# Row maxima 20 instead of 22 steps ahead of the scores, in an attention kernel with a dense gate

## The chip, the cores and the metric

The kernel runs on one core of one Trainium2 chip. The metric is the device time of one execution in microseconds. TensorE (PE), VectorE (DVE), ScalarE (ACT), GpSimd (POOL) and SyncE (SP, which only starts transfers here) have one instruction queue each, in program order.

## The reference

Attention with 32 query heads of 16 dimensions that share one key and value head, over a sequence of 2048, and beside it a layer of dense products with the Mish function; the output is a sum of x and the attention, gated.

```python
q = (x @ wq).reshape(B, S, H, Dh).transpose(0, 2, 1, 3)     # 32 heads, S = 2048, Dh = 16
k = x @ wk; v = x @ wv                                      # one head
p = softmax(einsum("bhqd,bkd->bhqk", q, k) * Dh ** -0.5)
o = einsum("bhqk,bkd->bhqd", p, v)                          # -> (S, 512) @ wo
h = einsum("bsd,df->bsf", x, w1) + b1                       # 512 -> 1792
act = h * tanh(softplus(h))                                 # Mish
y = einsum("bsf,fd->bsd", act, w2)                          # 1792 -> 512
```

A layernorm of x stands ahead of both, and the dense result passes a silu before it multiplies the attention's. All is float32, made of products of rounded high and low parts.

## The kernel before, in words

**Groups and steps.** The attention is cut into 32 groups `v` (four heads by 512 queries) of 16 steps each, `NS` = 512 steps in all. A step has four score products `e` (`score`, L1090), each followed by one exponential on ScalarE (`pts`, L1095), and four value products `pv` on the exponentials of the step before last (L1176; the profile counts eight matmuls for them). The scores use half of the array's rows at a time, half a=1 in even steps and a=0 in odd ones.

**Maxima.** The softmax needs the maximum of each row of scores before its exponentials. So the same scores are computed once more with queries and keys exchanged (`m_one`, matmul L1118), and VectorE takes the maximum of each 512 (reduce, L1122, into `mb`). A group has 64 such maxima products, 32 for each half of the array; each step carries four of them, for a later group. `LEAD` (L34) says how many steps they run ahead: ahead of the first score there must be 2 x `LEAD` maxima products on each half (L1436, and the end of the lead, L1498). `TAIL` = `NS` - `LEAD` is the step from which there are no maxima left. The tail takes the steps in pairs (`tail_pair`, L1590), with two dense groups side by side.

**The rows.** When a group's maxima are complete (`m_need`, L67), `c_rows` (L1134 to 1163) makes two more rows of its q tile out of them. It has pieces: a reduce (L1141), two small ones (`parts`), and a piece that transposes on VectorE (`turn`, L1151: `cr` out of `mp`) and then issues eight transfers of 2 KB on SyncE's queue (`move`, L1161: `qt<-cr`), four for half a=1 and then four for a=0. A group's first score (half a=1) waits for the first four, its fifth (the next step, half a=0) for the other four. `top_rows(n)` (L1567) queues up to n of these pieces: one behind each step, none behind a step that ended a dense group whose bank VectorE emptied (`top_rows(0 if evacs[0] else 1)`, L1733), two behind each half of a unit (L1679), three behind a pair of the tail (L1715).

**Dense work.** Beside these run dense products (queries of later groups, w1, w2, wo; L118 and L122, written to banks `xps`). Each is split into two halves of the array's rows, for two successive steps (`waves`): mostly six halves in a step, in some four or eight. A `unit` (L684) is four steps as two halves with a dense group of up to 16 products, ordered by the list `UNIT`.

**The lead.** All ahead of the first score is ordered by a planner (the loop of L1360 to 1560): it takes the task that can start first by its own costs, on each engine. `fill(n)` issues n dense products there, `keep_warm` a product whose result is not used; a task marked `fill` is preceded by such a product where no dense group is open. `cdone` is the time when the first group's rows are taken to be there, and ends the lead.

Of the kernel before, what the change touches and what calls it, by code (L numbers as in the profile page):

```python
# [30 lines left out]
NFT = F // P  # L31
NKT = S // P
NU = 8 * NC
LEAD = 22  # L34
NWARM = 24
E0 = 76.0
X_US = 9.0
# [91 lines left out]
def block_kernel(ctx: ExitStack, tc: tile.TileContext, x, wq, wk, wv, wo, w1, b1, w2, out):  # L129
# [10 lines left out]
    pe, act, dve, pool, sp = nc.tensor, nc.scalar, nc.vector, nc.gpsimd, nc.sync  # L140
# [46 lines left out]
    def f(ap):  # L187
        return ap.bitcast(F32)
# [354 lines left out]
    def pump():  # L543
        for tag in items:
            while arrived(tag):
                split(tag)
            for _ in range(2 if tag == "wb" else 1):
                load(tag)
# [135 lines left out]
    def unit(s, h):  # L684


        g, t = cur["g"], s + 2 * h
        xs = deque(g.mms)
        v, r = divmod(s, 16)
        es = deque((1 - h, r + j // 2, j % 2) for j in range(8))  # L690
        late = []
        relay = None

        def x_one():
            i = xs.popleft().half(cur["ps"], h)
            if len(xs) == len(g.mms) - 1 and h:
                tc.add_manual_dep(i.ins, cur["relay"].ins.name, mybir.DependencyInfo(
                    mybir.DependencyClass.Sync, mybir.DependencyReason.DATA), reason="other half of the bank")
            if h and g.dve and len(xs) == HOLD:
                held[0] = []  # L700
            if not xs and h:
                cur["n"] = len(g.mms)
                finish()
                for top in held[0] or ():
                    top()
                held[0] = None

        due(t)
        for n, op in enumerate(UNIT):
            if n == 8:  # L710
                due(t + 0.5)
                pump()
                due(t + 1)
            if xs:
                x_one()
            if op == "E":
                e = es.popleft()
                if len(es) > 1:
                    score(v, *e)()
                else:  # L720
                    late.append(score(v, *e))
            else:
                relay = m_one(1 - h)
        assert not xs and not es
        cur["relay"] = relay
        act_jobs(2 + (len(jobs) > 2))
        due(t + 1.5)
        for n in range(2):
            pv(t + n - 2)
            if n == 0:  # L730
                for fn in late:
                    fn()
        if t % 16 == 0:
            o_out((t - 16) // 16)
# [399 lines left out]
    def c_rows(v):  # L1134

        mp = sb.tile([P, 2, 3, 8], F32R, tag="mp", name=f"mp{v}", bufs=2)
        mx = f(mp[:, :, 0])
        w = {}

        def reduce():  # L1140
            dve.reduce_max(out=mx, in_=mb_of[v].rearrange("p b (a z) -> p a z b", a=2), axis=AX.X)  # L1141

        def parts():
            dve.tensor_reduce(out=mp[:, :, 1], in_=mx.rearrange("p a (z o) -> p a z o", o=1), axis=AX.X,
                              op=ALU.max, negate=True)
            dve.tensor_reduce(out=f(mp[:, :, 2]), in_=f(mp[:, :, 0:2]).rearrange("p a s z -> p a z s"), axis=AX.X,
                              op=ALU.add, negate=True)

        def turn():
            cr = w["cr"] = sb.tile([P, 32], F32, tag="cr", name=f"cr{v}", bufs=2)  # L1150
            dve.transpose(cr, f(mp[:, :, 1:3]).rearrange("p a s z -> p a (s z)"))  # L1151

        def move():
            q, cr = qt_of[v], w["cr"]
            if not lead:
                sp_t[0] = max(sp_t[0], us_of(step[0]) + 4.0)
            for a in range(1, -1, -1):
                r = 64 * a + 48
                for b in range(4):
                    sp_at(0.68)  # L1160
                    sp.dma_start(f(q[r:r + 2]).rearrange("o p (t b n) -> b o (p t) n", b=4, n=32)[b],  # L1161
                                 cr[32 * b + 16 * a:32 * b + 16 * a + 16])
        return reduce, parts, turn, move

# [102 lines left out]
    def due(t):  # L1267
        step[0] = t
        for k in sorted(k for k in timed if k <= t):
            for fn in timed.pop(k):  # L1270
                fn()
# [198 lines left out]
                   for d in k.deps)  # L1470

    begun = [0]
    cdone = [None]
    kind = [None]
    while True:
        opts = []
        for e in ("ACT", "DVE", "POOL", "SP"):
            if e == "POOL":
                T[e] = max(T[e], busy[0] + E0)
            if b := best(e):  # L1480
                early = max(now[0], b[1].start(0))
                opts.append((early if e == "DVE" and b[1].prio < 2 and b[0] < early + 5.0 else b[0], e, b[1]))
        b = best("PE")
        m = m_ready(T["PE"])
        if m is not None and b and b[0] < T["PE"] + 0.2 and T["DVE"] > T["PE"] + 1.0:
            m = None
        if m is not None and (b is None or m <= b[0] + 0.05 or T["DVE"] < T["PE"] + 0.3 and m <= T["PE"] + 0.1):
            opts.append((m, "PE", "M"))
        elif b:
            opts.append((b[0], "PE", b[1]))  # L1490
        e0 = min((o for o in opts if o[1] == "PE"), default=None, key=lambda o: o[0])
        low = min((o[0] for o in opts), default=None)
        if e0 is None or e0[0] > T["PE"] + 0.35:
            opts.append((T["PE"], "PE", "X"))
        if not any(o[1] == "ACT" and o[0] < T["ACT"] + 0.1 for o in opts):
            opts.append((T["ACT"], "ACT", "J"))
        s, e, k = min(opts, key=lambda o: o[0])
        if cdone[0] is not None and s >= cdone[0] - 0.4 and min(m_next) >= 2 * LEAD:  # L1498
            break
        when(s)  # L1500
        for tag in items:
            load(tag)
        if k == "M":
            d = max(T["DVE"], s + 0.45)
            for a in pick[0]:
                if m_next[a] == len(mseq):
                    mseq.append(pick[1])
                    got[pick[1][0]] += 1
                m_one(a)
                d += 0.6  # L1510
                m_ends.append(d)
            T["DVE"] = d
            T["PE"] = s + (0.25 if kind[0] == "M" else 0.45)
            kind[0] = "M"
            if vdone[0] == 0 and got[0] == 32 and m_next[0] == m_next[1]:
                vdone[0] = 1
                r = c_rows(0)
                r1 = task("DVE", 0.9, lambda: (r[0](), r[1](), r[2]()))

                def move():  # L1520
                    r[3]()
                    cdone[0] = now[0] + 4 * 0.65 + 2.0
                task("SP", 5.2, move, [r1])
        elif k == "X":
            fresh = cur["g"] is None
            if cur["g"] is not None or not waiting and (vdone[0] or begun[0] < 1 + (s - 18) / X_US) and begin():
                begun[0] += fresh
                fill(3)
                T["PE"] = s + 0.23 * 3 + (0.2 if kind[0] == "M" else 0)
                kind[0] = "X"  # L1530
            else:
                keep_warm()
                T["PE"] = s + 0.25
                kind[0] = "X"
        elif k == "J":
            tag = next((g for g in ("wq", "ws", "wb") if not any(soon(k, s) for k in plan["POOL"]) and arrived(g) and busy[0] + E0 < s + (4.5 if g == "ws" else 0.5)), None)
            n = ran[0]
            if tag:
                split(tag)
                T["ACT"] = s + 0.6  # L1540
            else:
                gap[0] = 0
                if not plan["POOL"]:
                    act_jobs(1)
                T["ACT"] = s + (0.65 if ran[0] > n else 0.15)
        else:
            plan[e].remove(k)
            if k.fill and cur["g"] is None and not waiting:
                keep_warm()
            k.fn()  # L1550
            T[e] = max(s, T[e]) + k.us + (0.15 if e == "PE" and kind[0] == "M" else 0)
            k.end = T[e]
            if e == "PE":
                kind[0] = "T"
# [117 lines left out]
    for s in range(NS + 2000):  # L1672
# [3 lines left out]
        if s % 4 == 0 and s + 4 <= NS - LEAD and unit_ready(s):  # L1676
            for h in range(2):
                unit(s, h)
                top_rows(2)  # L1679
                evacs[0] = 0  # L1680
                pump()
            base[:] = s + 4, us_of(s) + UNIT_US
            skip[0] = s + 4
            continue
# [66 lines left out]
```

## Time and profile before

| | |
|---|---|
| runs | 1563.36, 1560.67, 1563.7 us (median 1563.36) |
| the profiled execution | 1561.58 us |
| its span | 1559.8 us |
| TensorE busy | 1548.8 us (99%), mean granted clock 0.998 |
| VectorE, ScalarE, GpSimd busy | 1348.1, 1292.6, 636.3 us |
| first score of the attention | 80.23 us after the span's start |

The span is what the profile covers; 1.8 us of the execution lie around it. In a row of the profile stand the time or number, the engine, the kernel's line, the operation, and the tiles, output first (`e<-qt,ks` is a score product, `m<-ks,qt` a maxima product, `xps<-...` a dense one, `pv<-pts,vaug` a value product, `qt<-cr` the rows' transfers). What stands in brackets is the idle time before the row and what ended it.

### The profile page before, as it was taken

Reading aid. Unit: us, or ns where it says so; the run is one execution under the profiler, and the core shown is the slowest. Engines: PE = TensorE matmul, PEld = TensorE weight load, DVE = VectorE, ACT = ScalarE, POOL = GpSimd, SP = SyncE. Lnnn points to the kernel's source line nnn. Section 1 sums busy time; section 2 is a strip of 40 time slices with the busy share of each in tenths; the row PEclk is TensorE's granted clock in tenths of the full one; section 3 lists DMA queues with packets and bytes.
Section 4 is the critical chain, followed back from the end, with each engine's and each line's share of the span. In section 5 each row is a group of like instructions: output and inputs, shape, how many; then the busy total and the mean of one; then the engine's idle time right before and its main releaser. Section 6 shows DMA issues by size and latency. Waiting matters only on the chain.

```text
span 1559.8 us, 31423 instructions
## 1 busy us (share of the span) xinstructions
PE 1548.8 (99%) x11715; PEld 864.1 (55%) x11715; DVE 1348.1 (86%) x2280; ACT 1292.6 (83%) x2509; POOL 636.3 (41%) x668
## 2 busy tenths in 40 slices
PE   9999999999999999999999999999999999999998
PEld 6555655655555565565545556555554555655644
DVE  7998888889989988888998988888889999888854
ACT  6588888789888778977989788897788878878796
POOL 4787349366356203331625422163152323314122
PEclk9999999999999999999999999999999999999999
DMA  6334134133231303212113220321321213131020
GB/s 199 104 133 139 46 111 139 30 113 112 87 111 49 108 16 113 72 24 100 52 58 111 92 92 17 104 69 58 111 59 38 100 58 105 30 99 32 19 71 34
DMA packets 71955, 125.47 MB, mean 80 GB/s; under 512 B 19742, under 2 KB 33356, under 8 KB 71804
## 3 DMA queue, kind: packets, MB, share of 16 engines
q1 hardware_dynamic: 71372, 122.68, 24.9%
q8 instruction: 93, 1.52, 0.4%
q10 hardware_dynamic: 432, 0.79, 0.1%
q14 instruction: 58, 0.48, 0.1%
HBM read 75.57 MB, written 26.21 MB: 65 GB/s over the span
## 4 chain that ended last, share of the span: by engine, by line
PE 98%; DVE 1%; ACT 0%; DMA 0%; issue 0%
PE xps L122 45%; PE pv L1176 32%; PE m L1118 10%; PE e L1090 7%; PE xps L118 1%; DVE mb L1122 1%; PE warm L1344 1%; PE kp L356 0%; PE xp L315 0%; PE wop L122 0%; ACT pts L1095 0%; PE y2ps L122 0%; DMA ks<-ks 0%; PE wop L118 0%; ACT hb L808 0%; ACT xt L324 0%
## 5 line engine op out<-in xcount | busy, mean ns | idle before, releaser
L1122 DVE TENSOR_REDUCE mb<-m 128x1 f32<-128x512 f32 x2048 | 1266.2, 683 | 164.2 <-PE m L1118 129.0
L1095 ACT ACTIVATE pts<-e 128x512 f32<-128x512 f32 x2048 | 1064.8, 607 | 218.3 <-PE e L1090 164.0
L1118 PE MATMUL m<-ks,qt 48*128 48x512 f32 (+1 forms) x2048 | 842.3, 422 | 1.2 <-DMA ks<-ks 1.2
L1090 PE MATMUL e<-qt,ks 64*128 64x512 f32 x2048 | 750.9, 406 | 0.2 <-ACT pts L1095 0.2
L1176 PE MATMUL pv<-pts,vaug 128*32 128x512 f32 x4096 | 529.9, 603 | 0.0
L1118 PEld LDWEIGHTS m<-ks,qt 48*128 48x128 f32 (+1 forms) x2048 | 371.1, 185 | 79.5 <-DVE mb L1122 41.4
L1090 PEld LDWEIGHTS e<-qt,ks 64*128 64x128 f32 x2048 | 375.8, 186 | 29.9 <-ACT pts L1095 16.3
L122 PE MATMUL xps<-wbs,act 64*128 64x512 f32 x1270 | 324.6, 399 | 0.0
L122 PE MATMUL xps<-xt,ws 64*128 64x512 f32 x1128 | 312.3, 409 | 1.7 <-ACT pts L1095 0.9
L122 PEld LDWEIGHTS xps<-xt,ws 64*128 64x128 f32 x1128 | 194.4, 185 | 185.7 <-ACT pts L1095 123.3
L122 PEld LDWEIGHTS xps<-wbs,act 64*128 64x128 f32 x1270 | 227.0, 184 | 99.5 <-ACT pts L1095 26.8
L1176 PEld LDWEIGHTS pv<-pts,vaug 128*32 128x32 f32 x4096 | 88.3, 108 | 152.5 <-issue 144.5
L175 POOL TENSOR_TENSOR hb<-hb,t 128x512 f32<-128x512 f32 x56 | 72.2, 1289 | 163.2 <-ACT t L827 89.4
L185 POOL TENSOR_SCALAR t<-t 128x512 f32<-128x512 f32 x56 | 34.4, 614 | 181.5 <-ACT t L814 181.4
L122 PE MATMUL xps<-xt,wq 64*128 64x512 f32 x336 | 93.0, 409 | 0.0
L122 PEld LDWEIGHTS xps<-xt,wq 64*128 64x128 f32 x336 | 57.9, 185 | 55.4 <-ACT pts L1095 37.7
L175 POOL TENSOR_TENSOR oc<-oc,sc 128x512 f32<-128x512 f32 (+1 forms) x16 | 20.6, 1290 | 152.5 <-DMA qt<-qh 49.8
L122 PE MATMUL xps<-wbs,ot_all 64*128 64x512 f32 x288 | 79.3, 408 | 0.0
L122 PEld LDWEIGHTS xps<-wbs,ot_all 64*128 64x128 f32 x288 | 49.5, 184 | 46.9 <-ACT pts L1095 28.5
L175 POOL TENSOR_TENSOR act<-hb,act 128x512 fp32r<-128x512 f32 x56 | 72.1, 1288 | 4.7
L175 POOL TENSOR_TENSOR hb<-hb,u 128x512 f32<-128x512 f32 x56 | 72.2, 1289 | 4.4
L175 POOL TENSOR_TENSOR u<-u,t 128x512 f32<-128x512 f32 x56 | 71.9, 1284 | 4.7
(164 smaller groups left out, 878.6 us busy)
## 6 DMA issues: line engine op xcount, KB each, us to landing
wbs<-w SPq DMA_DIRECT2D x39, 512.0 KB
ws<-w SPq DMA_DIRECT2D x36, 512.0 KB
qt<-qh SPq DMA_DIRECT2D x256, 32.0 KB
w<-wbs SPq DMA_DIRECT2D x14, 512.0 KB
wq<-wq SPq DMA_DIRECT2D x14, 512.0 KB
wbs<-wo SPq DMA_DIRECT2D x12, 512.0 KB
rawws<-in_dram SPq DMA_DIRECT2D x20, 256.0 KB
w<-ws SPq DMA_DIRECT2D x10, 512.0 KB
```

Of the source, the lines that this page charges most:

```text
L118: self.pe.matmul(ps, self.lhs(), self.rhs(), start=(self.k == 0), stop=(self.k == self.tot - 1))
L122: i = self.pe.matmul(ps, self.lhs()[o], self.rhs()[o], start=(self.k == 0 and self.halves == 0), stop=(self.k == self.tot - 1 and self.hal ...
L175: eng.tensor_tensor(out=o, in0=a, in1=b, op=op)
L185: pool.tensor_scalar(o, o, lim, 0.0, op0=ALU.min, op1=ALU.max)
L1090: pe.matmul(e, ks[o:o + 64, P * k:P * (k + 1)], q[o:o + 64, p], start=True, stop=True)
L1095: x = act.activation(dst, e, AF.Exp, scale=0.25)
L1118: pe.matmul(m, q[o, p, P * t:P * (t + 1)], ks[o, C * kb:C * (kb + 1)], start=True, stop=True)
L1122: return dve.reduce_max(out=mb_of[v][:, kb, z:z + 1], in_=m, axis=AX.X)
L1176: pe.matmul(o[32 * j:32 * j + 32], vaug[:, k], pt, start=(k == 0), stop=(k == 15))
L1344: pe.matmul(warm, qts[0][:, 0, 0:P], qts[0][:, 0], start=True, stop=True)
```

## The change

`LEAD` becomes 20. In a unit a row piece is queued in the middle of each half, and behind the half one or none, where there were two behind it. Of the first group's transfers for half a=1, two are issued on ScalarE's queue. The planner of the lead takes these rows to be there earlier, opens its first dense group with three, two and one products, and issues one product ahead of each marked task until 27 us if a dense group is open.

```diff
-LEAD = 22
+LEAD = 20
...
@@ unit
             if n == 8:
                 due(t + 0.5)
+                top_rows(1)
                 pump()
...
@@ c_rows, move
-                    sp.dma_start(f(q[r:r + 2]).rearrange("o p (t b n) -> b o (p t) n", b=4, n=32)[b],
+                    (act if lead and a and b % 2 else sp).dma_start(f(q[r:r + 2]).rearrange("o p (t b n) -> b o (p t) n", b=4, n=32)[b],
                                  cr[32 * b + 16 * a:32 * b + 16 * a + 16])
...
@@ the lead's planner
+    fills = deque((3, 2, 1))
...
-                    cdone[0] = now[0] + 4 * 0.65 + 2.0
-                task("SP", 5.2, move, [r1])
+                    cdone[0] = now[0] + 2 * 0.65 + 2.0
+                    T["ACT"] = max(T["ACT"], now[0]) + 2.5
+                task("SP", 3.9, move, [r1])
...
-                fill(3)
+                n = fills.popleft() if begun[0] == 1 and fills else 3
+                fill(n)
...
-            if k.fill and cur["g"] is None and not waiting:
+            if k.fill and cur["g"] is not None and s < 27.0:
+                fill(1)
+            elif k.fill and cur["g"] is None and not waiting:
                 keep_warm()
...
@@ the loop over the steps, units
                 unit(s, h)
-                top_rows(2)
+                top_rows(0 if evacs[0] else 1)
                 evacs[0] = 0
```

What it does to the order is shown at two places. The first is the start of group 10, on TensorE and VectorE. In a row, `m_1_11` is maxima product 11 on half a=1 (here of group 11, whose q tile is `qt_79`), `e_15_1_0` a score of key block 15 on half a=0 (the last of group 9), and `e_0_0_1` the first score of group 10 (q tile `qt_78`). TensorE before:

```order
2568 L1118 MATMUL m_1_11_7566<-ks,qt_79 128x512
2569 L1090 MATMUL e_15_1_0_7569<-qt_77,ks 128x512
2570 L1176 MATMUL pv_7077<-pts,vaug 32x512 x4
2571 L122 MATMUL xps<-wbs,act_0_4025 128x512
2572 L1118 MATMUL m_1_12_7580<-ks,qt_79 128x512
2573 L122 MATMUL xps<-wbs,act_0_4025 128x512
2574 L1090 MATMUL e_0_0_1_7584<-qt_78,ks 128x512
```

And TensorE after:

```order
2539 L1119 MATMUL m_1_7_7502<-ks,qt_79 128x512
2540 L1091 MATMUL e_15_1_0_7505<-qt_77,ks 128x512
2541 L1177 MATMUL pv_7015<-pts,vaug 32x512 x4
2542 L122 MATMUL xps<-xt_2985,ws_6565 128x512
2543 L1119 MATMUL m_1_8_7516<-ks,qt_79 128x512
2544 L122 MATMUL xps<-xt_2985,ws_6565 128x512
2545 L1091 MATMUL e_0_0_1_7520<-qt_78,ks 128x512
```

The group's first score stands behind maxima product 12 of half a=1 before, behind number 8 after. VectorE around the transpose that makes group 10's rows, before:

```order
809 L1122 TENSOR_REDUCE mb_7347<-m_1_6_7439 128x1
810 L1122 TENSOR_REDUCE mb_7347<-m_0_4_7446 128x1
811 L1151 STREAM_TRANSPOSE cr_7457<-mp_7344 128x32
812 L1122 TENSOR_REDUCE mb_7347<-m_0_5_7470 128x1
813 L1122 TENSOR_REDUCE mb_7347<-m_0_6_7478 128x1
```

And after:

```order
809 L1123 TENSOR_REDUCE mb_7355<-m_1_6_7446 128x1
810 L1123 TENSOR_REDUCE mb_7355<-m_0_4_7453 128x1
811 L1152 STREAM_TRANSPOSE cr_7463<-mp_7350 128x32
812 L1123 TENSOR_REDUCE mb_7355<-m_0_5_7474 128x1
813 L1123 TENSOR_REDUCE mb_7355<-m_0_6_7482 128x1
```

The transpose stands behind the same maximum in both, while the score moved up by four maxima of each half: 13 maxima products stand between the two before (m_0_5 to m_0_11 and m_1_7 to m_1_12), five after (m_0_5 to m_0_7, m_1_7 and m_1_8).

The second place is the end of the lead on TensorE. `m_0_8` here is a maxima product of group 1; the single `xps` products of L122 belong to the first step. Before:

```order
130 L118 MATMUL xps<-xt_175,ws_833 128x512 x3
131 L1118 MATMUL m_0_8_955<-ks,qt_78 128x512
132 L1118 MATMUL m_1_8_958<-ks,qt_78 128x512
133 L1118 MATMUL m_0_9_963<-ks,qt_78 128x512
134 L1118 MATMUL m_1_9_966<-ks,qt_78 128x512
135 L118 MATMUL xps<-xt_175,ws_833 128x512 x6
136 L1118 MATMUL m_0_10_982<-ks,qt_78 128x512
137 L1118 MATMUL m_1_10_985<-ks,qt_78 128x512
138 L1118 MATMUL m_0_11_988<-ks,qt_78 128x512
139 L1118 MATMUL m_1_11_991<-ks,qt_78 128x512
140 L118 MATMUL xps<-xt_175,ws_833 128x512 x3
141 L122 MATMUL xps<-xt_175,ws_920 128x512
```

And after:

```order
132 L1119 MATMUL m_1_7_932<-ks,qt_78 128x512
133 L118 MATMUL xps<-xt_175,xtw 128x512 x6
134 L118 MATMUL xps<-xt_175,ws_833 128x512 x12
135 L1432 MATMUL warm<-qt_79 128x512
136 L122 MATMUL xps<-xt_175,ws_920 128x512
137 L1119 MATMUL m_1_8_972<-ks,qt_78 128x512
138 L122 MATMUL xps<-xt_175,ws_920 128x512
139 L1091 MATMUL e_0_0_1_976<-qt_77,ks 128x512
```

The last eight maxima products of the lead are gone from it (products 8 and up of group 1 now belong to the first steps), and one `keep_warm` product has come. Over the whole program the number of instructions is the same on each engine, but for that product, the two transfers on ScalarE's queue and one more instruction on GpSimd.

## Prediction

> **What bounds the kernel now.** I read the page first: the busy row, the shares of the chain that ended last, and the costliest group of VectorE.
>
> ```profile
> PE 1548.8 (99%) x11715; PEld 864.1 (55%) x11715; DVE 1348.1 (86%) x2280; ACT 1292.6 (83%) x2509; POOL 636.3 (41%) x668
> PE 98%; DVE 1%; ACT 0%; DMA 0%; issue 0%
> L1122 DVE TENSOR_REDUCE mb<-m 128x1 f32<-128x512 f32 x2048 | 1266.2, 683 | 164.2 <-PE m L1118 129.0
> ```
>
> TensorE is busy 1548.8 of 1559.8 us, and the chain stays on it. Nothing else ends last anywhere of note. So the change can gain only by dropping TensorE work (it drops none: the same score, maxima, value and dense products are in both programs), by packing it better, or out of the 11 us in which TensorE is idle. It can lose wherever TensorE now waits.
>
> Next the chain in order of time (start, us, engine, line). Each step ends in eight value products, so the distance of two such rows is the length of a step: first a step with four dense halves, then steps with six, six and eight, then half of a unit (two steps, 16 halves).
>
> ```profile
> 399.89 1.00 PE pv L1176 x8
> 402.59 1.00 PE pv L1176 x8
> ...
> 534.15 0.99 PE pv L1176 x8
> 537.00 1.00 PE pv L1176 x8
> 539.87 0.99 PE pv L1176 x8
> 542.93 0.99 PE pv L1176 x8
> ...
> 164.81 1.85 PE pv L1176 x16
> 170.80 1.85 PE pv L1176 x16
> ```
>
> So 2.70 us with four halves, 2.85 and 2.87 with six, 3.06 with eight, 5.99 for half of a unit.
>
> **What the change can break: the way of a group's rows.** A group's 64 maxima end in a transpose on VectorE, which makes the rows `cr`. SyncE then sends them to the q tile in eight transfers, four for the half a=1 of the array, then four for a=0. The group's first score needs the first four. The timeline of group 10, before:
>
> ```profile
> 532.47 0.20 DVE L1151 STREAM_TRANSPOSE cr<-mp 128x32 f32<-128x32 f32 x1
> 532.70 5.32 SPq L1161 DMA_DIRECT2D qt<-cr  x8
> ...
> 541.13 0.40 PE L1090 MATMUL e<-qt,ks 64*128 64x512 f32 x1
> ```
>
> From turn to first score there are 8.66 us, which hold three whole steps and a remainder. With two steps fewer (2.85 and 2.87) it would be 2.94 us. How long the rows need, I read at group 5, whose rows cross half of a unit; the fourth issue stands in a row of its own, and the reduces beside it are three in 1.88 us.
>
> ```profile
> 306.17 0.20 DVE L1151 STREAM_TRANSPOSE cr<-mp 128x32 f32<-128x32 f32 x1
> 306.40 5.29 SPq L1161 DMA_DIRECT2D qt<-cr  x8
> ...
> 308.47 0.61 SPq L1161 DMA_DIRECT2D qt<-cr  x1
> 308.57 1.88 DVE L1122 TENSOR_REDUCE mb<-m 128x1 f32<-128x512 f32 x3
> ...
> 313.12 0.40 PE L1090 MATMUL e<-qt,ks 64*128 64x512 f32 x1
> ```
>
> An issue takes 5.29 / 8 = 0.66 us, and the fourth begins 2.30 us after the turn. When its bytes move is in the windows of stretches (the last two columns are the share of the DMA engines and GB/s; the clock of TensorE is ahead of them). When TensorE could run after a transfer shows only at the lead's `ks` copies, where it waited for one.
>
> ```profile
> 309.70:309.85 0.15, 0.15 (x5) 0.15 (x2) 0.15 (x2) 0.15 (x1) 0.00 (x0) 1.00 0.09 14
> 309.85:310.30 0.45, 0.45 (x7) 0.36 (x6) 0.45 (x1) 0.45 (x2) 0.00 (x0) 1.00 0.00 0
> 61.00:61.35 0.35, 0.00 (x0) 0.00 (x0) 0.35 (x2) 0.00 (x0) 0.35 (x1) 1.00 0.17 50
> 61.35:61.80 0.45, 0.00 (x0) 0.00 (x0) 0.45 (x1) 0.00 (x0) 0.45 (x2) 1.00 0.00 0
> ```
>
> ```profile
> 58.57 1.15 SPq L372 DMA_DIRECT2D ks<-ks  x2
> ...
> 61.84 0.70 PE L1118 MATMUL m<-ks,qt 64*128 64x512 f32 x3 [1.19 <-DMA ks<-ks]
> ```
>
> The rows' fourth transfer moves its bytes up to 309.85, 3.68 us after the turn. The `ks` bytes ended at 61.35 and TensorE ran at 61.84, 0.49 us later. So I put the earliest first score at turn + 4.17 us. The ends: turn + 3.68 (no delay behind the bytes) and turn + 4.99 (issue to restart as with `ks`: its second issue begins at about 58.57 + 0.58 = 59.15, 2.69 us before 61.84; 2.30 + 2.69 = 4.99).
>
> **The change part by part.** *Maxima 20 steps ahead.* The program orders say how many maxima stand between the turn and the group's first score. Before it is 17 (four steps) in most groups, 13 in groups 7, 10 and 18, and 9 (half of a unit) in 5, 11, 13, 19 and 30. After, 19 groups have 9 (two steps, or half of a unit); groups 7, 10, 14, 16, 18, 22, 24, 25 and 26 have 5 (one step), since a step in which VectorE also empties a dense bank queues no piece; and 5 and 30 have 5 in the middle of a unit. Groups 0 and 31 are apart and keep their room. Then:
>
> - One step between: 2.94 in hand against 4.17 needed, a wait of 1.23 us on TensorE; nine of them make 11.1. Group 10 is typical, and all nine lie in single steps.
> - Middle of a unit: by group 5's rows the second of the three reduces ends at 308.57 + 1.25 = 309.82, five maxima ahead of the score at 313.12. That is 3.3 in hand, a wait of 0.87; two make 1.7.
> - Two steps between: 2.94 + 2.85 = 5.8 in hand, 1.6 more than needed. No wait. The fifth score wants the other four transfers, which end four issues (2.6 us) later, but it stands a step (2.85) later: no second wait.
>
> Behind the waiting score TensorE holds everything: its queue is in order, so maxima, dense and value products stand still, and VectorE and ScalarE run dry. Nothing makes that up, as the steps behind are TensorE's own (99%). The sum of the waits is 12.8 us. With the ends it is 9 x 0.74 + 2 x 0.38 = 7.4 and 9 x 2.05 + 2 x 1.69 = 21.8. I take the middle value, since its 0.49 us is the only delay from bytes to TensorE that the trace has.
>
> By the Trainium skill ("DMA: Bandwidth & Descriptors", the section on the anatomy of one DMA, written for the gpsimd path) a transfer costs a fixed 2.0 us or so, mostly the wait for the receipt. With that the fourth would be done at 308.47 + 2.0, turn + 4.3, and the waits would be about 1.36 and 1.0, 14.2 us in all instead of 12.8; the rows agree within that.
>
> *The lead's end.* Eight maxima fewer stand ahead of the first score. The first group's rows go out at 73.05, and the rows of TensorE there are:
>
> ```profile
> 73.05 5.34 SPq L1161 DMA_DIRECT2D qt<-cr  x8
> ...
> 75.21 0.73 PE L1118 MATMUL m<-ks,qt 64*128 64x512 f32 x4
> 75.88 1.66 PE L118 MATMUL xps<-xt,ws 128*128 128x512 f32 x6
> 77.47 0.73 PE L1118 MATMUL m<-ks,qt 64*128 64x512 f32 x4
> 78.13 0.97 PE L118 MATMUL xps<-xt,ws 128*128 128x512 f32 x3
> ...
> 80.23 0.39 PE L1090 MATMUL e<-qt,ks 64*128 64x512 f32 x1
> ```
>
> The two lots of four took 75.88 - 75.21 + 78.13 - 77.47 = 1.33 us, and the changes of kind beside them go too: I take -1.5 (ends -1.9, with some more of such changes, and -0.2, if ScalarE's two new issues, 2 x 0.66, hold back an activation that TensorE needs). The two queues bring the a=1 rows in 1.3 us earlier, which is worth nothing: with one queue they were ready about 73.05 - 0.23 + 4.17 = 77.0, over 3 us ahead of 80.23, and the score now stands at some 78.7. "Early dense products" moves dense work within the lead and adds none: 72 products of the first dense layer stand ahead of the first score in both programs. One warm-up product more is some 0.1 us.
>
> *The main stage.* The eight maxima come back here, in two more steps. By the orders: 64 halves of units for 62, 331 steps of six for 333, none of eight for four, and four with no dense half, which the trace doesn't have. Such a step I put at 2.65: at least 2.34 (2.70 less four halves at (3.06 - 2.70) / 4 = 0.09), at most the 2.85 of six; VectorE's four reduces at 0.63 to 0.68 make 2.5 to 2.7. Sum: 2 x 5.99 - 2 x 2.85 - 4 x 3.06 + 4 x 2.65 = +4.6 (3.4 to 5.4).
>
> *The tail.* It loses one pair of steps. Its lengths, by the chain: a pair that is not short of ScalarE takes 4.44, one with 13 dense halves 5.02.
>
> ```profile
> 1507.68 1.85 PE pv L1176 x16
> 1512.12 1.85 PE pv L1176 x16
> ...
> 1529.98 1.85 PE pv L1176 x16
> 1535.00 1.85 PE pv L1176 x16
> ```
>
> Before there are two of 13, after two of 18 and one short pair fewer. Eighteen halves are 5.02 plus five at 0.11 to 0.21, 5.6 to 6.1: I take 6.1, so 2 x 6.1 - 2 x 5.02 - 4.44 = -2.3 (down to -3.3).
>
> Without the waits the sum is -1.5 + 4.6 - 2.3 = +0.8, as it must be near nothing where the work is the same. With them it is +13.6: the profiled execution (span 1559.8, time 1561.58) becomes 1575.2. It lay 1.8 under the median of the runs, 1563.36, so the median would be up to 1577.0. I say 1576.
>
> **The rivals.** *No wait comes.* The rows would have to be in by the time of the score: a turn queued earlier than the order says, VectorE further ahead, or time made up behind the wait. Then the sum is +0.8 and the time 1563 to 1564. Against it: VectorE cannot run ahead of TensorE's maxima, and the turn stands behind the same maximum in both programs. That also covers a change that doesn't do what it says, as with the dense products; I give 0.08 to the waits being hidden, and 0.03 to a gain of over 3 us from better packing beside hidden waits (1560).
>
> *The 19 groups with two steps wait as well.* They have 1.6 us in hand. A transfer of half a megabyte ahead of the rows would use it up:
>
> ```profile
> GB/s 199 104 133 139 46 111 139 30 113 112 87 111 49 108 16 113 72 24 100 52 58 111 92 92 17 104 69 58 111 59 38 100 58 105 30 99 32 19 71 34
> ```
>
> At the best slice's 199 GB/s 512 KB take 2.6 us; a wait of 1.0 in 19 groups, and 2.6 more in some of the others, gives +33 at the most, +19 more being the likelier: 1594. Against: SyncE's first issue came 0.23 us behind the turn in both groups shown, and the fourth's bytes moved 1.38 us after its issue began. Chance 0.05.
>
> *The clock falls in the waits.* Eleven waits, each followed by a step at half speed, cost 11 x 2.85 = 31 us: 1606. The only wait of this kind that the trace has, 1.19 us, shows none of it in the windows around it:
>
> ```profile
> 59.70:61.80 2.10, 0.95 (x5) 0.42 (x3) 2.10 (x4) 0.63 (x1) 2.02 (x3) 1.00 0.41 142
> 61.80:65.00 3.20, 3.14 (x15) 1.82 (x15) 2.71 (x6) 0.60 (x1) 2.96 (x4) 1.00 0.00 0
> ```
>
> The granted clock is 1.00 in and after it. Chance 0.02. The Trainium skill ("TensorE: Matmul & The Clock Gate", on HAM oscillation) sets the danger at gaps over some 3.4 us; by that rule too our 1.2 us would do nothing, and the trace agrees.
>
> **How the numbers follow.** Forecast 0.82, waits hidden 0.08, a gain 0.03, more waits 0.05, the clock 0.02. The forecast's own ends: lead, main, tail and waits at their lowest are -1.9 + 3.4 - 3.3 + 7.4 = +5.6, or 1567.2; at their highest -0.2 + 5.4 - 2.3 + 21.8 = +24.7, or 1586.3. The runs scatter by a microsecond or two around the profiled execution and not all terms are at one end together, so 1566 to 1585 holds eight in ten; the hidden waits lie below it and the rest above. A measurement of this kernel can tell about 0.2% (3.1 us) from no change: hidden waits are "same" save for a part, the small gain is "faster", and the forecast and the others are "slower".
>
> **What would show it.** In the profile after: TensorE's rows of `e<-qt,ks` with idle time released by DMA `qt<-cr`, about 1.2 us each, in nine groups and shorter in two; none in the other groups; the distance of value products there some 4.1 instead of 2.85; TensorE's busy share down to 98%, its busy time the same; the first score at some 78.7. Wrong it is if those rows carry no wait, if the waits are much longer than 1.3 us (the completion was mis-sized), or if groups with two steps wait.

## The result and the profile after

The changed kernel takes 1571.6 us in the median of six runs (1571.24 to 1572.97), against 1563.32 before (six runs, 1560.31 to 1563.7). The ratio is 1.0066, with a 95% interval of 1.0056 to 1.0076: slower by 0.66%, or 8.3 us between the medians. The profiled execution took 1572.08 us, span 1570.3, that is 10.5 us of span more than before (1559.8). The runs of before scatter more than those of after, and in the later comparisons the scatter goes with the granted clock: of their 54 runs those at 0.996 took 1563.4 to 1563.9 us and those at 0.999 or 1.000 took 1559.8 to 1560.7, so that the median of before lies at 1560.4 to 1561.4 there. So I follow the spans.

From the page after: the busy row, the chain's shares, and the row of the score products, whose last part is the idle time ahead of them.

```profile
PE 1551.3 (99%) x11716; PEld 864.6 (55%) x11716; DVE 1347.4 (86%) x2280; ACT 1292.7 (82%) x2508; POOL 636.9 (41%) x669
...
PE 93%; DVE 3%; SPq 1%; DMA 1%; ACT 1%; issue 0%; DVEq 0%
...
L1091 PE MATMUL e<-qt,ks 64*128 64x512 f32 x2048 | 750.1, 406 | 6.9 <-DMA qt<-cr 5.8
```

SyncE's queue and the DMA `qt<-cr` stand in the chain now, at 1% each, and the scores wait for them, where before nothing of the kind was. How one such wait comes about is read best from the chain in order of time, at group 10:

```profile
536.69 0.68 DVE mb L1123
537.37 0.13 DVE cr L1152
537.50 0.02 issue
537.52 0.68 SPq L1162
538.20 0.05 issue
538.25 0.66 SPq L1162
538.90 0.05 issue
538.96 0.61 SPq L1162
539.57 0.04 issue
539.61 1.66 DMA qt<-cr
541.27 0.14 issue
541.41 0.47 PE e L1091
```

The maximum, the transpose, three issues of some 0.66 us, then the fourth transfer, 1.66 us from the start of its issue to its completion, and 0.14 us later the score. The transpose began at 537.29, so the score stands at turn + 4.12. On TensorE the same place looks like this:

```profile
539.03 1.07 PE L1177 MATMUL pv<-pts,vaug 128*32 128x512 f32 x8
...
541.41 0.47 PE L1091 MATMUL e<-qt,ks 64*128 64x512 f32 x1 [0.65 <-DMA qt<-cr]
...
542.99 1.06 PE L1177 MATMUL pv<-pts,vaug 128*32 128x512 f32 x8
```

From one lot of value products to the next are 3.96 us where a step of six halves took 2.85 or 2.87. The idle time in brackets, 0.65, is less than the 1.1 us that the step has lost: a product's row lasts until its modelled end, and the products issued ahead of the wait cover a part of it. So the price of a wait is read from the length of the step, and not from the idle time.

The whole span is divided in the same way, at the first score, which ends the lead, and at the first scores of the tail. After:

```profile
77.88 0.39 PE L1091 MATMUL e<-qt,ks 64*128 64x512 f32 x1
...
1509.57 0.50 PE L1091 MATMUL e<-qt,ks 64*128 64x512 f32 x2
```

And before, where the first score stood at 80.23:

```profile
1495.42 0.50 PE L1090 MATMUL e<-qt,ks 64*128 64x512 f32 x2
```

| stretch | before | after | difference | forecast |
|---|---|---|---|---|
| to the first score | 80.23 | 77.88 | -2.35 | -1.5 |
| first score to the tail | 1415.19 | 1431.69 | +16.50 | +4.6 + 12.8 |
| the tail, to the end of the span | 64.38 | 60.73 | -3.65 | -2.3 |
| span | 1559.8 | 1570.3 | +10.5 | +13.6 |

In the middle stretch the steps that begin groups 7, 10, 14, 16, 18, 22, 24, 25 and 26 are together 10.2 us longer than others of their kind (1.0 to 1.2 each, group 7 1.4; group 22 begins in a unit), and the halves of units that begin groups 5 and 30 1.3 us. That is 11.5; 5.0 are left for the two steps more. The profile puts nine of these eleven waits down to `qt<-cr` (5.8 us of idle time in all). At groups 22 and 30 it puts the idle time, 0.59 and 0.32 us, down to `issue`, but their scores stand at turn + 4.05 and + 4.14 like the others.

### The profile page after: what moved, and what is told of

Its sections match the earlier page's. It is cut to its first block, busy times and chain, and to the rows that moved or that the text cites. A ratio compares the mean times of both kernels' runs of the same rounds, so it can differ in the third digit from the quotient of the medians.

```text
span 1570.3 us, 31413 instructions
## 1 busy us (share of the span) xinstructions
PE 1551.3 (99%) x11716; PEld 864.6 (55%) x11716; DVE 1347.4 (86%) x2280; ACT 1292.7 (82%) x2508; POOL 636.9 (41%) x669
## 4 chain that ended last, share of the span: by engine, by line
PE 93%; DVE 3%; SPq 1%; DMA 1%; ACT 1%; issue 0%; DVEq 0%
PE xps L122 43%; PE pv L1177 31%; PE m L1119 10%; PE e L1091 7%; DVE mb L1123 3%; PE xps L118 1%; SPq L1162 1%; DMA qt<-cr 1%; PE warm L1345 1%; PE wop L122 0%; PE kp L356 0%; ACT pts L1096 0%; PE xp L315 0%; PE y2ps L122 0%; PE wop L118 0%
## 5 line engine op out<-in xcount | busy, mean ns | idle before, releaser
L122 PE MATMUL xps<-wbs,act 64*128 64x512 f32 x1270 | 325.1, 399 | 0.0
L122 PE MATMUL xps<-xt,ws 64*128 64x512 f32 x1128 | 313.2, 410 | 1.5 <-ACT pts L1096 1.0
L122 PEld LDWEIGHTS xps<-xt,ws 64*128 64x128 f32 x1128 | 194.0, 185 | 184.9 <-ACT pts L1096 123.2
L122 PEld LDWEIGHTS xps<-wbs,act 64*128 64x128 f32 x1270 | 226.4, 184 | 95.1 <-ACT pts L1096 23.5
L122 PE MATMUL xps<-xt,wq 64*128 64x512 f32 x336 | 93.0, 409 | 0.0
L122 PEld LDWEIGHTS xps<-xt,wq 64*128 64x128 f32 x336 | 57.9, 185 | 55.3 <-ACT pts L1096 37.7
L122 PE MATMUL xps<-wbs,ot_all 64*128 64x512 f32 x288 | 79.5, 408 | 0.0
L122 PEld LDWEIGHTS xps<-wbs,ot_all 64*128 64x128 f32 x288 | 49.4, 184 | 46.5 <-ACT pts L1096 28.5
L170 POOL TENSOR_SCALAR qh<-ql 128x512 fp32r<-128x512 f32 x15 | 9.3, 620 | 115.1 <-ACT ql L751 115.0
```

The lines of the kernel that those rows point to most:

```text
L122: i = self.pe.matmul(ps, self.lhs()[o], self.rhs()[o], start=(self.k == 0 and self.halves == 0), stop=(self.k == self.tot - 1 and self.hal ...
L170: pool.tensor_scalar(o, i, 1.0, 0.0, op0=ALU.mult, op1=ALU.add)
```

## The experiments

**A piece behind every step.** If the late rows are the cause, they must go when the turn is queued on time.

```diff
-                top_rows(0 if evacs[0] else 1)     # behind a half of a unit
+                top_rows(1)
...
-        top_rows(0 if evacs[0] else 1)             # behind a step
+        top_rows(1)
```

> The changed kernel, but a row piece is queued behind every step, also behind one in which VectorE empties a dense bank. By the order every group then has nine maxima (two steps) or more between its turn and its first score; all else keeps its place. Theory (the rows come too late in eleven groups): no TensorE wait on qt<-cr is left, the span falls by the 11.5 us that the nine long steps and the two halves of units carry, from 1570.3 to about 1559, the median to 1560 or 1561 (1558.5 to 1563). Rival one (the shorter lead packs the main stage and the tail worse, the waits only show it): the time stays within 3 us of 1571.6. Rival two (a piece beside the emptying of a bank holds TensorE up): the waits go, but the steps that end a dense group grow by some 0.5 us each, and 1566 or more is left.

It took 1561.97 us (eleven runs, 1561.68 to 1562.9), 1.0007 of before (0.9998 to 1.0016), span 1560.4. The first rows of TensorE's waits, of the changed kernel and of this one:

```profile
PE e L1091 <- DMA qt<-cr: 5.8, 9, 0.9
PE m L1119 <- DVE mb L1123: 2.6, 6, 0.8
```

```profile
PE m L1119 <- DVE mb L1123: 2.5, 9, 0.7
PE warm L1345 <- DVE one L197: 2.0, 1, 2.0
```

The waits on `qt<-cr` are gone and 9.9 of the 10.5 us of span with them. So the slowdown is the late rows; the shorter lead and tail are worth nothing by themselves, as the sum without the waits had it (+0.8). The second rival is right in a small way: seven steps that end a dense group and now hold a piece too are 0.3 to 0.4 us longer than other steps; without the piece it was about 0.15. Leaving the piece out there saved some 0.2 us and cost a wait of 1.1.

**Rows later by whole issues.** Here the a=1 transfers are pushed back by one, two, three or all four of the a=0 ones, so that the suspected wait grows in steps of 0.66 us and the work stays the same. The order of the issues, with n from 1 to 4 (written here for all four alike; the lines between are left out):

```diff
-            for a in range(1, -1, -1):
-                for b in range(4):
+            for a, b in [(0, b) for b in range(n)] + [(1, b) for b in range(4)] + [(0, b) for b in range(n, 4)]:
```

All four:

> The changed kernel, but the four transfers for half a=0 are issued ahead of the four for a=1, in every group. The first score's rows are then four issues (2.64 us) later: 4.12 + 2.64 = 6.76 us after the turn. Theory (the fourth transfer of a=1 sets the first score): the eleven groups that wait already wait 2.64 us longer each (+29), and some 14 groups with two single steps between (5.8 us in hand) now wait 0.9 to 1.0 us (+13): 1571.6 + 42 = 1614 (1605 to 1622), with first scores at turn + 6.7 to 6.8. Rival (the wait is of something else that goes with the turn, such as VectorE's queue): first scores stay at turn + 4.1 and the time within 5 us of 1571.6. Rival (the clock falls in waits of over three microseconds): the steps behind the long waits run slower, 1625 or more and a granted clock below 0.99.

It took 1636.76 us (one run). First scores of the eleven stand at turn + 6.6 to 7.1, about as worked out (group 10: 551.49 and 558.21), and sixteen more groups wait, not 14, with steps longer by 0.7 to 1.3 us. The waits alone would give +44; there are 65. The rest is the clock. The score of group 10 and the windows around it (the clock is the third figure from the end):

```profile
558.21 0.70 PE L1091 MATMUL e<-qt,ks 64*128 64x512 f32 x1 [3.26 <-DMA qt<-cr]
```

```profile
552.00:554.40 2.40, 2.40 (x22) 1.17 (x19) 2.40 (x4) 2.26 (x5) 0.60 (x1) 1.00 0.04 9
554.40:558.10 3.70, 0.55 (x3) 0.11 (x3) 0.70 (x2) 0.29 (x1) 1.29 (x2) 1.00 0.02 3
558.10:559.50 1.40, 1.29 (x6) 1.26 (x8) 0.12 (x1) 0.55 (x1) 0.00 (x0) 0.56 0.98 269
559.50:561.00 1.50, 1.50 (x11) 0.78 (x8) 1.34 (x3) 0.99 (x3) 0.00 (x0) 0.50 0.24 98
561.00:562.60 1.60, 1.60 (x11) 0.47 (x12) 0.52 (x1) 0.74 (x2) 0.00 (x0) 0.78 0.00 0
562.60:564.50 1.90, 1.90 (x18) 1.24 (x18) 1.63 (x3) 1.40 (x3) 0.00 (x0) 1.00 0.00 0
```

The granted clock falls to one half at the end of the wait and stays there for some three microseconds. The same befell ten of the eleven long waits, and brought some 2 us each. So the rival on the clock holds, but for waits three times those of the changed kernel. One issue later:

> The changed kernel, but one of the four transfers for half a=0 is issued ahead of the four for a=1 in every group: the rows for the first score come one issue (0.66 us) later. Theory: first scores at turn + 4.8 in the eleven groups that wait, whose waits grow by 0.66 us each to 1.8 in all, 0.66 x 11 = +7 us: 1579 (1577 to 1581). The groups with two steps (5.8 in hand) still don't wait. The clock keeps up, as TensorE is idle for under two microseconds. Rival (the waits were not of the issues): no change, 1571.6.

1578.83 us (one run): +7.2 for 7.3 forecast, with eleven waits and a clock of 1.000. The eleven steps themselves are 19.0 us too long in the sum, where it was 11.5: 7.5 more. Up to here the price is the wait and nothing else. Three issues later:

> As before, with three of the a=0 transfers ahead: 1.98 us later, first scores at turn + 6.1, waits of 3.15 us in eleven groups and of 0.3 in some 14 with two single steps. By the waits alone 1571.6 + 11 x 1.98 + 14 x 0.3 = 1597.6. With all four ahead the steps behind a wait of 3.8 us took 5.2 to 6.4 us longer, 1.4 to 2.6 more than the wait. If the clock falls only from a certain length of idle time on, somewhere between 1.2 and 3.6 us, this one tells where it lies: idle rows of some 2.6 us with no further loss mean 1596 to 1599, with the further loss of some 2 us for each of eleven 1615 to 1622.

1612.75 us (one run), nearer to the upper case: the nine groups with idle rows of 2.57 to 2.95 us lose a further 1.4 to 3.0 us each, some of it in the step behind; groups 5 and 30, idle for 2.2 us, lose nothing more. At group 10:

```profile
550.12 0.47 PE L1091 MATMUL e<-qt,ks 64*128 64x512 f32 x1 [2.61 <-DMA qt<-cr]
```

```profile
547.60:550.10 2.50, 0.00 (x0) 0.01 (x1) 0.44 (x1) 0.00 (x0) 0.74 (x1) 1.00 0.02 3
550.10:551.50 1.40, 1.38 (x11) 1.11 (x11) 0.63 (x2) 0.87 (x2) 0.00 (x0) 0.99 0.59 174
551.50:553.00 1.50, 1.50 (x11) 0.20 (x8) 1.26 (x3) 1.20 (x3) 0.00 (x0) 0.50 0.50 188
553.00:554.30 1.30, 1.30 (x6) 0.50 (x4) 0.00 (x0) 0.00 (x0) 0.00 (x0) 0.50 0.00 0
```

Here the clock falls 1.4 us after TensorE has gone on. Two issues later:

> The changed kernel with two of the a=0 transfers ahead of the four for a=1: rows 1.32 us later than in the changed kernel, first scores at turn + 5.45, idle rows of some 1.9 to 2.3 us in nine groups and 1.5 in two; groups with two single steps (5.8 in hand) don't wait. With idle rows up to 1.7 us nothing came on top of the wait, with 2.6 to 3.0 us the clock fell to one half for some 3.3 us, and two rows of 2.2 us (in units) didn't bring that. If the fall needs more than some 2.3 us idle: 1571.6 + 11 x 1.32 = 1586 (1584 to 1588), clock 1.0. If it comes with some of them already: 1 to 2 us more for each, up to 1602, and a clock below 0.998.

1597.32 us (one run), clock 0.991, where the waits alone give 1586. I had thought of a length of idle time from which the clock falls, and that is not so. Here it fell behind eight of the eleven waits. At group 5 it fell after an idle row of 1.54 us, and at group 25 it stayed after one of 1.96. What tells them apart is where the wait lies on a fixed beat. The trace keeps the time of every change of the granted clock: in each of these runs all changes stand whole multiples of 3.413 us apart, and each stretch at one half lasts 3.413 us or twice that, but for the last, which the end cuts off. Both scores, and the stretches of 3.41 us on this run's beat around each:

```profile
310.74 0.47 PE L1091 MATMUL e<-qt,ks 64*128 64x512 f32 x1 [1.54 <-DMA qt<-cr]
1261.73 0.47 PE L1091 MATMUL e<-qt,ks 64*128 64x512 f32 x1 [1.96 <-DMA qt<-cr]
```

```profile
308.62:312.03 3.41, 1.86 (x15) 1.34 (x17) 1.23 (x2) 0.94 (x3) 0.00 (x0) 1.00 0.02 3
312.03:315.44 3.41, 3.41 (x20) 2.92 (x17) 2.72 (x5) 2.48 (x5) 0.00 (x0) 0.50 0.00 0
315.44:318.85 3.41, 3.41 (x29) 1.46 (x27) 1.78 (x4) 1.80 (x4) 0.00 (x0) 1.00 0.00 0
...
1257.52:1260.94 3.42, 2.25 (x17) 0.74 (x13) 2.42 (x4) 2.09 (x5) 0.00 (x0) 1.00 0.02 3
1260.94:1264.35 3.41, 2.62 (x21) 1.33 (x21) 1.87 (x3) 2.11 (x5) 0.00 (x0) 1.00 0.37 123
```

Over the four kernels the clock never fell with the rows one issue later (idle up to 1.71 us), fell behind eight waits of eleven with two issues (idle 1.54 to 2.44), behind nine of eleven with three, and ten of eleven with four, where group 30 got through an idle row of 2.87. So a longer wait makes it likelier, and no single length decides.

What goes with a fall is how much of one such stretch TensorE's rows fill (the first figure behind the length). Group 5's wait lies in one stretch, filled to 0.55, and the next stretch is at one half throughout. Group 25's wait, though longer, is shared by two, filled to 0.66 and 0.77, and the clock stays. Cut in this way from the first score to 15 us ahead of the end, the traces of all twelve kernels hold 28 falls from the full clock. The clock fell behind each of the 24 stretches filled to less than 0.5, and behind none that was filled to 0.58 or more. Of the seven between 0.52 and 0.57 it fell behind four. With the rows one issue later the emptiest stretch had 0.59, in the changed kernel 0.78. The beat starts at another place in each execution, so whether a wait is cut in two is chance. This is read from traces of other experiments, and no run was made to test it; the ends of TensorE's rows are modelled, so the shares are rough. Ahead of the first score the reading fails: in the kernel before the clock fell at 24.84 us behind a stretch that the rows fill.

**The transfers on two queues in every group.**

```diff
-                    (act if lead and a and b % 2 else sp).dma_start(
+                    (act if a and b % 2 else sp).dma_start(
```

> The changed kernel, but the pieces b=1 and b=3 of half a=1 go out on ScalarE's queue in every group, not only in the first. Each queue then issues two of the four. Theory: the last of them is issued 0.23 + 0.66 us after the turn instead of 2.30, so the first score could run at about turn + 2.7, within the 2.94 in hand: the eleven waits go (-11.5). ScalarE gets 62 more issues, which stand in its queue behind the turn: if they cost it some 0.66 us each where it is late already, up to 20 us come back. 1560 to 1575, and with the waits on qt<-cr gone in most groups. Rival (the time from issue to landing, not the row of four issues, is what counts): waits of about 1.2 us stay, 1571 or more.

1586.65 us (four runs, 1.0166 of before, 1.0153 to 1.018): the waits on `qt<-cr` go, but the kernel is slower than with them. I had 1575 as the upper end. The first row of TensorE's waits, and ScalarE at group 10:

```profile
PE e L1091 <- ACT pts L1096: 14.7, 28, 1.5
```

```profile
545.30 1.28 ACTq L1162 DMA_DIRECT2D qt<-cr  x2
546.63 1.08 ACT L1096 ACTIVATE pts<-e 128x512 f32<-128x512 f32 x2 [1.70 <-PE e L1091]
```

ScalarE's two issues take 1.28 us, ahead of exponentials whose banks TensorE needs back. Nearly every group pays 0.9 us in the step of its turn, also the 19 that never waited: some 28 us for the 11.5 saved. ScalarE, busy for 82%, had no 1.3 us to give in one place. Both queues issue two of the four, the last at turn + 0.96, which with 1.80 us would be in time for the 3.0 in hand. But the longer step alone put the scores off to turn + 4.0, nearly late enough for rows from one queue (4.1), so this run doesn't show that the second queue ended the waits. The clock fell once here too, behind a wait of 1.45 us for ScalarE at group 5.

**The changed units alone, 22 steps ahead.** The edit is the kernel before with the two lines of `top_rows` in the units.

> The kernel before (22 steps ahead, its own lead) with only the change of the row pieces in units: one in the middle of each half, one or none behind it. Every group has nine maxima or more between turn and first score. Theory (only the lack of steps costs): no wait on qt<-cr, the time of before, 1563 (1560 to 1565). Rival (a piece in the middle of a unit's half holds VectorE and so the unit up): the 62 halves grow by 0.05 us or more, 1566 or more.

1563.06 us (ten runs), 1.002 of before (1.0011 to 1.0029), no wait on `qt<-cr`. The 62 halves of units are 2.6 us longer in the sum than before's (means 6.020 and 5.978), short of the rival's figures, but more than the theory's nothing. It is not spread over all: the halves that hold a group's pieces are 0.3 longer. The change to the units costs 2 or 3 us by itself at 22 steps, an edit that the prediction had not priced. With 20 steps and a piece behind every step the same count gives a mean of 5.996, some 1 us in all.

**The first rows on one queue.** From the kernel with a piece behind every step:

```diff
-                    (act if lead and a and b % 2 else sp).dma_start(
+                    sp.dma_start(
```

> The kernel with a piece behind every step, with all eight transfers of the first group's rows on SyncE's queue again. Theory (these rows were not last at the lead's end; the activation and the bank are): the first score within 0.5 us of where it stands with two queues, allowing for the scatter of the lead (76.9 and 77.9 in two executions), the time the same, 1562 (1560.5 to 1563.5). Rival (the two queues bring the first score forward by the two issues saved): 1.3 us longer, the first score with an idle row released by qt<-cr.

1561.94 us (ten runs, 1.0004 of before, 0.9995 to 1.0013), the first score at 77.0 for 76.88 with two queues. The two-queue edit is worth nothing, as forecast.

**Pieces made good.** In place of one piece less behind a step that ends a dense group, two behind the next, and the turn never left out:

```diff
+    def step_rows():
+        if evacs[0] and len(rowq) != 1:
+            owed[0] = 1
+            top_rows(0)
+        else:
+            top_rows(1 + owed[0])
+            owed[0] = 0
```

> The changed kernel, but where a piece is left out behind a step that ends a dense group, the next step gets two, and the turn itself is never left out. By the order every group has nine maxima or more, as with a piece behind every step, and only the turn may stand beside the emptying of a bank. Theory: the waits on qt<-cr stay away, and the seven steps that were 0.3 to 0.4 us long with a piece beside the emptying become shorter: 1560 to 1562, at most 2 us under the kernel with a piece behind every step. Rival (two pieces in one step hold VectorE up by more): 1562 to 1565.

1560.73 us (eleven runs), 0.9998 of before (0.9989 to 1.0007), span 1558.6. No wait on `qt<-cr`, and the steps of 0.3 to 0.4 us excess are down to 0.14. It is the best version with 20 steps, faster than the changed kernel by 11 to 12 us of span, and not to be told from the kernel before.

**Without the early dense products.** From the kernel just above:

```diff
-    fills = deque((3, 2, 1))
+    fills = deque((3, 3, 3))
...
-            if k.fill and cur["g"] is not None and s < 27.0:
+            if k.fill and cur["g"] is not None and s < 0.0:
```

> The kernel of the pieces made good, with the lead's two dense edits undone (the first group opens with three products, no single product ahead of a marked task before 27 us). Theory (they move products within the lead and add none): the first score within 0.5 us of 76.6, the time within 1 us of 1560.7. Rival (they fill time in which TensorE would idle): the first score 1 us later or more, 1562 or more.

1561.45 us (ten runs, 1.0001 of before, 0.9992 to 1.0011). The first score stands at 77.61 for 76.57: later by 1.0, as the rival has it, with the wait for `ks<-ks` of 1.2 us back; the time is 0.7 us more, less than the rival's 1.3 and within what these runs scatter. By the spans (1559.7 and 1558.6) the early products would be worth about 1 us, but nine executions with them have their first score anywhere from 76.50 to 77.88, and 77.61 lies within that. What does repeat is TensorE's idle time ahead of the maxima that need the `ks` copy: 0.63 to 0.87 us in these nine, 1.16 to 1.19 in the three without (before, the changed units alone, and this one). So half a microsecond is shown, and the rest is open.

## Why the prediction was right, and where its sizes were off

**The mechanism** held at every point: the rows are late in the eleven groups that the order named and in no other, the nineteen groups with two steps don't wait, and nothing makes the wait up. The first score at turn + 4.17 was measured at + 4.05 to + 4.20. Only that all nine lie in single steps was wrong: group 22 begins in a unit, at about the same price.

**The waits** were put at 12.8 and are 11.5. A single step lost 1.1 where 1.23 was forecast, since the time in hand was 3.0 for 2.94 and the completion came 0.05 sooner; the halves of units lost 0.65 and 0.7 for 0.87. The later rows by one issue gave back the price of the wait to 0.1 us, so this term is shown and not only fitted.

**The completion** of a small transfer was borrowed from the `ks` copy's 0.49 us between the end of the bytes and TensorE. The chain after has 1.66 from issue to completion and 0.14 to TensorE, 1.80 in all, where the forecast had 4.17 - 2.30 = 1.87. That a delay read at another copy fits so well is partly luck: from issue to restart that copy took 2.69 us, and by that the waits would have been 21.8 us. The 2.0 us of the Trainium skill ("DMA: Bandwidth & Descriptors", the section on the anatomy of one DMA), written for the gpsimd path, would have been 0.2 too long for these 2 KB on SyncE's queue.

**The lead** gave 2.35 for 1.5. In its last stretch it is 1.73 (from 74.31 to 80.23 before, 73.69 to 77.88 after); 0.6 comes from further ahead, where the early dense products cover part of the `ks` copy. "Worth nothing" was wrong there by about half a microsecond.

**The main stage** cost 5.0 for 4.6, with the pieces in units, unpriced, within it.

**The tail** gave 3.65 for 2.3. This term was mis-sized: two pairs of 18 halves were put at 6.1 each, and the chain after has them at 5.19 and 5.18:

```profile
1544.63 1.85 PE pv L1177 x16
1549.82 1.85 PE pv L1177 x16
...
1555.00 3.57 PE pv L1177 x32
```

I had worked from a pair of 13 at 5.02 and 0.2 us a half. But 14 halves in a row, both halves of the array side by side, take 1.74 us, 0.12 each.

**The rivals.** Hidden waits: out, the waits stand in the trace. More groups waiting: out. The clock: out at these lengths, with 1.000 granted in the profiled execution, but the reason that I gave was too weak. The Trainium skill ("TensorE: Matmul & The Clock Gate", on HAM oscillation) sets the danger at gaps of over some 3.4 us, and with the rows two issues later the clock fell behind idle rows between 1.54 and 2.44 us. Here the trace doesn't agree with the rule. The changed kernel, whose longest is 0.92, was nearer to a fall than the rule says: with one issue more a stretch was filled to 0.59 only, and 0.57 was once too little.

**The offset.** 1576 was the sum on the profiled execution, 1575.2, and some of the 1.8 us by which that execution lay under the median. After, the profiled execution lay 0.5 over its median, so that part was scatter. The sum itself was 3.1 us too high: the waits by 1.3, the lead by 0.85 and the tail by 1.35 came out lower than forecast, and the main stage by 0.4 higher.

## What to carry to other kernels

Count, for each result that comes by a transfer, the work that stands between its last producer and its first reader in the reader's queue, and set it against issue times plus completion: here 2.30 + 1.80 us against one step's 3.0. Shortening a lead spends just this margin, and a rule that now and then leaves a piece of the chain out ("not beside an emptied bank") has to be tested against the smallest margin, not the usual one. Work moved to a second queue is free only where that engine has the issue time to spare at that very place.

## What the runs showed of the hardware

The granted clock of TensorE changed on a beat of 3.413 us in every run in which it changed more than once, and fell to one half for one or two beats. With the rows two to four issues later it fell behind idle rows as short as 1.54 us, up to 1.8 us after TensorE had gone on and sometimes while it still waited; rows of 1.96, 2.21 and 2.87 us passed without it. From the first score on it always fell behind a stretch of the beat that TensorE's rows filled to less than half, and never behind one filled to 0.58 or more. A fall cost 1.4 to 1.6 us beside the wait where it lasted 3.413 us, and 2 to 3 us where it lasted twice that.

At group 10 of the changed kernel a transfer of 2 KB on SyncE's queue took 0.61 to 0.68 us to issue, the fourth was complete 1.66 us after its issue began, and the waiting product began 0.14 us later. Two such issues on ScalarE's queue took 1.28 us of ScalarE's time.
